# Beta in four loads spread by TensorE, L written in three operations, and conversions moved behind the rounds, in a DeltaNet and SwiGLU kernel

## The chip, the cores and the metric

The kernel runs on one core of a Trainium2 chip, as one program. The metric is the time of one execution in device microseconds (us); lower is better. The engines are named as in the profile: PE (TensorE; PEld is its loading of stationary operands), DVE (VectorE), ACT (ScalarE), POOL (GpSimd) and SP (SyncE). SP issues nearly all transfers; ACT and POOL can issue them too, each in the order of its own instructions.

## The reference, cut to what matters

The first part is a linear recurrence over 768 positions for 4 batches of 8 heads of 48 dimensions; its output, turned to 3072 tokens of 384 features, goes through a gated feed-forward block.

```python
k_n = k / (np.linalg.norm(k, axis=-1, keepdims=True) + 1e-06)
for t in range(S):
    kt, vt, bt = (k_n[:, :, t], v[:, :, t], beta[:, :, t, None])
    y[:, :, t] = np.einsum('bhd,bhde->bhe', q[:, :, t], state)
    v_old = np.einsum('bhde,bhd->bhe', state, kt)
    state = state + bt[:, :, :, None] * np.einsum('bhd,bhe->bhde', kt, vt - v_old)
...
g = x @ w_gate
silu = g * (1.0 / (1.0 + np.exp(-g)))
val = x @ w_val
return (silu * val @ w_out).astype(np.float32)
```

Everything is FP32. `beta` has one number for each batch, head and position.

## The kernel before, in words

The 768 positions are worked in 12 chunks of 64. Within a chunk the recurrence becomes a triangular system: with L the strict lower triangle of K K^T, scaled by Beta over the norms, the chunk's updates are the solution of that system. Chunks are treated in pairs, called groups. Groups 1 to 5 invert their diagonal blocks by a substitution of 31 steps on DVE (`substitute`). Group 0, chunks 0 and 1, comes first and has its own functions, which the change is about.

The order of the work is written out by hand (`tc.manual_schedule`, L1539): what stands earlier in the text is issued earlier on its engine, and each engine keeps that order. For the start it is this.

- K of chunks 0 and 1 is loaded, half by SP and half by ACT (L186, L187). `load_beta` (L383) is then called 16 times (L1549 to L1551): each loads 8 heads for one block of 32 positions of either chunk straight to the 8 lanes (partitions) that use it, with 672 numbers a lane, of which later steps read every fourth block of 32. Eight of these go out on POOL, four on ACT and four on SP.
- `first_tiles` (L553) clears L's tile and makes masks. `norms` (L359) sums squares of K.
- SP goes on with Q of chunk 0, K of 2 and 3, Q of 1, V of 0 and the first weights (L1556 to L1565).
- `unread` (L577) issues 100 products of one column, whose results nobody reads.
- `turned` (L420) makes K^T: eight transposes on PE (L444) and two copies on ACT (L446). It is called for chunk 0 and chunk 1, and then `first_gram` (L584) makes K K^T of both. For each of 32 pairs of head and batch it issues two products: the upper 32 rows against their own 32 columns (L592), and the lower 32 rows against all 64 (L593).
- `first_diag` (L596) copies diagonal blocks out, half by ACT and half by DVE; ACT copies Beta into place (L1573); DVE turns the blocks over (L1577) and `first_scale` (L612) multiplies by Beta over the norms, with POOL and DVE.
- `first_substitution` (L625) inverts diagonal blocks of 16 in 15 steps of two DVE operations (L637, L643). `first_z` (L645) and `spread_z` (L650) put the result, Z, where PE reads it.
- Meanwhile ACT runs `low_copies` (L600) for chunks 0 and 1: the part of L outside the diagonal blocks, six operations a chunk on 32 lanes each (L605, L610). PE turns Q of chunks 0 and 1 and K of 2 and 3 and makes their products (L444, L458); ACT copies results.
- `advance(0)` then runs: N = L times Z (L667), the first solution (L876), and three rounds (L896). A round multiplies by N in two halves (two parities of the heads) and adds on DVE (L1260). After that come the outputs (L932, or L896 again for chunk 0), the turning into tokens (L989, L992) and the new state (L944, L956).

The weights arrive in pieces and are rewritten before PE uses them: ACT makes two operations of each piece (`power_step`, L257) and DVE three (`convert`, L273: L282, L290, L302). The first gate products need pieces 0, 2 and 4, the first value products pieces 1, 3 and 5. Before, each of the six halves of the rounds is followed by the conversion of one of these pieces (L1615 to L1617). From L1634 on the feed-forward products of chunks 0 and 1 follow, with the rest of the conversions between them (`chain`, L1627), and from chunk 2 on a loop with fewer products a chunk (`gate_val_fast`, `output_fast`).

Of the kernel before, what the change touches and what calls it, by code (L numbers as in the profile page):

```python
# [13 lines left out]
C = 64  # L14
# [6 lines left out]
def kernel(  # L21
# [201 lines left out]
    place_of += [("z1", H_ * n) for n in (2, 3, 1, 0)]  # L223
    place_of += in_wo + in_work + (in_z1 + in_work) * 3

    beta_s = places["wo"].bitcast(FP32)[:, 6 * H_ : 6 * H_ + NG * 128]
    LATE = {"zb": 18, "p_sb": 12}
    freed_by = {}
    for n, (name, lo) in enumerate(place_of):
# [150 lines left out]
                out=beta_b[:, g], in0=beta_b[:, g], in1=r_n, op=ALU.mult  # L380
            )

    def load_beta(at, queue=nc.gpsimd):  # L383

        s_, blk, c, par = at // 8, at // 4 % 2, at // 2 % 2, at % 2
        lo, m = 64 * c + R * blk, (NG - 1) * 128 + R
        queue.dma_start(
            out=beta_s[8 * at : 8 * at + 8, 0:m],
            in_=beta.rearrange("(b bp) (j par) s -> b par bp j s", b=2, par=2)[
                s_ ^ par, par, :, :, lo : lo + m  # L390
            ],
        )

    def first_n():
        n = n_t[0].rearrange("p c h -> p (c h)")
# [157 lines left out]
    def first_tiles():  # L553
        a = work.tile([128, C * 2 * HH], FP32, name="a_sb")
        for c in range(2):
            l_sb[c] = a[:, R * R * c : R * R * (c + 1)].rearrange(
                "p (h k) -> p h k", k=C
            )
        first_of["flat"] = new_mb().rearrange("p k i -> p (k i)")
        first_of["diag"] = first_of["flat"].rearrange("p (j h) -> p h j", j=R)  # L560
        first_of["zb"] = places["z1"].bitcast(FP32)[:, 4 * H_ - 1056 : 4 * H_]
        first_of["mb"] = places["wo"].bitcast(FP32)[:, 2 * H_ : 2 * H_ + 1056]
        nc.vector.memset(first_of["zb"], 0.0)
        nc.vector.memset(a, 0.0)
        for x, rows in enumerate((slice(16, C), slice(R, C), slice(48, C), slice(0, R))):
            nc.vector.tensor_reduce(
                out=m_two[:, x],
                in_=ident.rearrange("p (b n) -> p b n", b=2)[:, :, rows],
                axis=mybir.AxisListType.X,
                op=ALU.add,  # L570
            )
        nc.vector.tensor_tensor(
            out=m_rows, in0=m_two[:, :, 0], in1=m_two[:, :, 1], op=ALU.add
        )
        nc.vector.tensor_scalar_mul(m_low, m_rows[:, 0:3], -1.0)

    def unread():  # L577

        p = ps_pair("p_t", "px")[:, 0]
        for n in range(100):  # L580
            q_ = QUADS[n % 4][0]
            nc.tensor.matmul(p[q_, 0:1], ident[q_, q_], ident[q_, 0:1])

    def first_gram(c, tag):  # L584

        p_g = ps_pair("p_g", tag)
        p_v = p_g.rearrange("p par (x h i) -> p par x h i", x=2, i=R)
        for bp, j, par, b, _ in every():
            k_v = kt[c][half_of(par), bp, j, b].rearrange("p (x i) -> p x i", x=2)
            h, s_ = NJ * bp + j, b ^ par  # L590
            hi, lo = slice(64 * s_, 64 * s_ + R), slice(64 * s_ + R, 64 * s_ + C)
            nc.tensor.matmul(p_v[hi, par, 1, h], k_v[:, 0], k_v[:, 0])  # L592
            nc.tensor.matmul(p_v[lo, par, :, h], k_v[:, 1], k_v)  # L593
        return p_v

# [3 lines left out]

    def low_copies(c, p):  # L600
        l_v = l_sb[c].rearrange("p (par h) k -> p par h k", par=2)
        for s_ in range(2):
            hi, lo = QUADS[2 * s_][0], QUADS[2 * s_ + 1][0]
            for rows, x in ((hi, 0), (lo, 2)):
                nc.scalar.mul(  # L605
                    l_v[rows, :, :, B16 * x : B16 * x + B16],
                    p[rows, :, 1, :, 0:B16],
                    m_low[rows, x : x + 1],
                )
            nc.scalar.mul(l_v[lo, :, :, 0:R], p[lo, :, 0], -1.0)  # L610

    def first_scale(r_b):  # L612
        zb, b = first_of["zb"], beta_b[:, 0]
# [925 lines left out]
    with tc.manual_schedule(  # L1539
        engines={  # L1540
            mybir.EngineType.PE,
            mybir.EngineType.Activation,
            mybir.EngineType.DVE,
            mybir.EngineType.SP,
            mybir.EngineType.Pool,
        }
    ):
        new_n(0)
        for at in range(0, 16, 2):  # L1549
            load_beta(at)  # L1550
            load_beta(at + 1, nc.sync if at % 4 else nc.scalar)  # L1551
        first_tiles()
        norms(0)

        norms(1)
        load_q(0)  # L1556
        load_k(2)
        load_k(3)
        load_q(1)
        load_v(0)  # L1560
        for n in range(12):
            stage(n)
        load_v(1)
        stage(12)
        stage(13)  # L1565
        copy_a, copy_v = nc.scalar.copy, nc.vector.tensor_copy
        unread()
        turned(0, False)
        turned(1, False, "py")
        p_g = [first_gram(0, "px"), first_gram(1, "py")]  # L1570
        first_diag(0, 0, p_g[0], copy_a)
        first_diag(0, 1, p_g[0], copy_v)
        copy_a(beta_b, beta_s.rearrange("p (g r) -> p g r", g=NG)[:, :, 0:R])  # L1573
        first_diag(1, 0, p_g[1], copy_a)
        r_b = first_n()
        first_diag(1, 1, p_g[1], copy_v)
        nc.vector.transpose(first_of["mb"][:, 0 : R * R], first_of["flat"])  # L1577
        first_scale(r_b)
        low_copies(0, p_g[0])
        turned(0, True, 0)  # L1580
        low_copies(1, p_g[1])
        turned(2, False, "px")
        first_q = [gram_steps(0, True, 2)]
        next(first_q[0])
        turned(3, False, "py")
        turned(1, True, 0)
        gram(2, False, "px", (copy_a, copy_a))
        gram(3, False, "py", (copy_a, copy_a))
        first_q.append(gram_steps(1, True, 0))
        next(first_q[1])  # L1590
        first_substitution()
        for n in range(14, 18):
            stage(n)
        first_z()
        for n in range(18, 23):
            stage(n)
        some, others = slice(0, HH // 2), slice(HH // 2, HH)
        spread_z(0, 1, nc.scalar, some)
        spread_z(0, 0, nc.vector)
        spread_z(0, 1, nc.vector, others)  # L1600
        scale_v(0)
        for steps_of in first_q:
            next(steps_of)
        new_nt(0, qpad[1].rearrange("p bp h d -> p (bp h d)"))
        zb_1 = work.tile([128, R, R], FP32, name="zb", bufs=1)
        new_nt(1, zb_1.rearrange("p k i -> p (k i)"))
        step("advance", advance, 0)
        power_step(0)
        power_step(2)
        for x in range(2):  # L1610
            spread_z(1, x, nc.scalar)
            power_step((4, 1)[x])
        power_step(3)
        power_step(5)
        for n in (0, 2, 4, 1, 3, 5):  # L1615
            step("advance", advance, 0)
            converts_first(n)  # L1617
        step("advance", advance, 0)
        p_n = banks("p_n", "px")
        n_products(1, p_n, (0,))  # L1620
        step("advance", advance, 0)
        n_products(1, p_n, (1,))
        scale_v(1)
        for par in range(2):
            n_copy(1, p_n, par)

        def chain(at):  # L1627

            step("advance", advance, 0 if steps("advance", 0) < 4 else 1)
            converts(1 + (at + 1) % 2)  # L1630

        pairs = [(c, f) for c in range(2) for f in range(0, 8, 2)]
        pairs += [(c, f) for f in range(8, FT, 2) for c in range(2)]
        for at, (c, f) in enumerate(pairs):  # L1634
            early = c == 0 and f < 4
            if c == 1 and f == 0:
                finish(1)
                second_inverse.append(invert(1))
                for _ in range(3):
                    next(second_inverse[0])  # L1640
            elif not early:
                point(2)
            need((6, 12, 18, 24, 30, 30)[f // 2])
            gate_val(c, f, fill, at, chain if early else None)
        need(len(pieces))
        for bp in range(NB):
            point(2)
            output(0, bp, fill, (4, 8))
        output(1, 0, fill, (4, 8))
        hold.clear()  # L1650
        first_blocks(True)
        first_blocks(False)
        point(2)
        output(1, 1, fill, range(2, FT, 2))
        finish(2)
        x_sums(2)
        sums_of_w(12)
        for c in range(2, NCH):
            if c > FAST:
                begin(c, 0)  # L1660
            point(c + 1)
            if c == FAST:
                begin(c, 0)
            for r in range(ROUNDS):
                gate_val_fast(c, r, fill)
            output_fast(c, fill)
            finish(c + 1)
            x_sums(c + 1)
# [30 lines left out]
```

## Time and profile before

| what | value |
|---|---|
| time, median of 4 runs | 707.93 us (706.82 to 710.69) |
| the profiled execution, its own time | 706.82 us |
| its span | 705.1 us |
| PE busy | 682.7 us, 97% of the span, 11,440 matmuls |
| DVE, ACT, POOL busy | 473.5, 261.7, 52.9 us |
| first product of the rounds (L896) begins | 37.05 us |
| first gate product (L1189) begins | 52.05 us |

The profile is one execution. Its span runs from the first instruction to the last; the time contains 1.7 us more. "Idle before" is the time an engine stood before an instruction, with what ended it behind the arrow. A matmul in FP32 shows as two pairs of LDWEIGHTS and MATMUL. In the stretch tables the columns are length, busy time of PE, PEld, DVE, ACT and POOL, each with the number of instructions in brackets, then the granted clock of PE as a share of full speed, the busy share of the DMA engines and GB/s.

### The profile page before, as it was taken

Reading aid. Unit: us, or ns where it says so; the run is one execution under the profiler, and the core shown is the slowest. Engines: PE = TensorE matmul, PEld = TensorE weight load, DVE = VectorE, ACT = ScalarE, POOL = GpSimd, SP = SyncE. Lnnn points to the kernel's source line nnn. Section 1 sums busy time; section 2 is a strip of 40 time slices with the busy share of each in tenths; the row PEclk is TensorE's granted clock in tenths of the full one; section 3 lists DMA queues with packets and bytes.
Section 4 is the critical chain, followed back from the end, with each engine's and each line's share of the span. In section 5 each row is a group of like instructions: output and inputs, shape, how many; then the busy total and the mean of one; then the engine's idle time right before and its main releaser. Section 6 shows DMA issues by size and latency. Waiting matters only on the chain.

```text
span 705.1 us, 25711 instructions
## 1 busy us (share of the span) xinstructions
PE 682.7 (97%) x11440; PEld 643.1 (91%) x11440; DVE 473.5 (67%) x1092; ACT 261.7 (37%) x548; POOL 52.9 (8%) x46
## 2 busy tenths in 40 slices
PE   6689999999999999999999999999999999999997
PEld 5688888756899999999999999999999999999997
DVE  6865689798899848987458787379855345333342
ACT  3656676203543433335223235142153132142220
POOL 7000020205000030000300000300000000000000
PEclk9889999999999999999999999999999999999999
DMA  8982716004661422365333174154141141211210
GB/s 132 249 213 70 198 48 220 1 23 84 190 128 33 99 64 70 76 113 108 67 82 82 42 131 102 26 121 85 49 106 53 30 94 61 53 63 46 68 46 23
DMA packets 144111, 62.57 MB, mean 89 GB/s; under 512 B 123136, under 2 KB 126208, under 8 KB 144000
## 3 DMA queue, kind: packets, MB, share of 16 engines
q1 hardware_dynamic: 141600, 60.27, 36.2%
q8 instruction: 90, 1.47, 0.9%
q10 hardware_dynamic: 2144, 0.48, 0.5%
q0 software_dynamic: 256, 0.17, 0.1%
q14 instruction: 21, 0.17, 0.1%
HBM read 53.82 MB, written 7.08 MB: 86 GB/s over the span
## 4 chain that ended last, share of the span: by engine, by line
PE 92%; ACT 2%; DVE 2%; issue 2%; DMA 1%; SPq 0%; DVEq 0%; ACTq 0%
PE ffn L1093 43%; PE ffn L1299 20%; PE ffn L1189 8%; PE ffn L1216 4%; PE p_g L458 3%; PE p_u L876 2%; PE p_s L944 2%; PE p_r L838 2%; PE p_y L932 1%; PE p_y L847 1%; DMA kn<-in_k_dram 1%; PE p_f L989 1%; PE ffn L896 1%; PE p_u L896 1%; PE p_j L801 1%
## 5 line engine op out<-in xcount | busy, mean ns | idle before, releaser
L1093 PE MATMUL ffn<-x_ffn,wg_sb 128*128 128x128 f32 x840 | 128.3, 275 | 0.4 <-ACT x_ffn L992 0.2
L1093 PE MATMUL ffn<-x_ffn,wv_sb 128*128 128x128 f32 x840 | 128.1, 275 | 0.0
L1093 PEld LDWEIGHTS ffn<-x_ffn,wg_sb 128*128 128x128 f32 x840 | 111.1, 192 | 0.7 <-ACT ffn L1149 0.3
L1093 PEld LDWEIGHTS ffn<-x_ffn,wv_sb 128*128 128x128 f32 x840 | 110.7, 192 | 0.0
L1123 ACT ACTIVATE sil<-ffn 128x256 f32<-128x256 f32 x120 | 46.0, 383 | 132.8 <-PE ffn L1093 128.1
L1299 PE MATMUL ffn<-wo_sb,h_f 128*128 128x192 f32 x480 | 83.4, 327 | 0.0
L1128 DVE TENSOR_TENSOR h_f<-sil,ffn 128x256 f32<-128x256 f32 x120 | 49.5, 418 | 48.6 <-ACT sil L1123 46.3
L1299 PEld LDWEIGHTS ffn<-wo_sb,h_f 128*128 128x128 f32 x480 | 78.1, 190 | 0.4
L1260 DVE TENSOR_TENSOR ffn<-ffn,p_sb 128x512 f32<-128x512 f32 x58 | 40.3, 695 | 44.3 <-ACT ffn L1149 43.2
L1093 PE MATMUL ffn<-x_t,h_f 128*128 128x128 f32 x480 | 61.1, 280 | 0.2 <-ACT ffn L1106 0.2
L1093 PEld LDWEIGHTS ffn<-x_t,h_f 128*128 128x128 f32 x480 | 56.2, 191 | 1.4 <-ACT ffn L1106 0.4
L536 DVE TENSOR_TENSOR zb<-zb,tmp 128x31 f32<-128x31 f32 (+15 forms) x155 | 53.1, 343 | 5.3
L746 POOL TENSOR_TENSOR n_b<-mb,half 128x32 f32<-128x32 f32 x5 | 30.0, 6001 | 342.8 <-DVE mb L500 342.8
L530 DVE TENSOR_TENSOR tmp<-zb,mb 128x31 f32<-128x31 f32 (+15 forms) x155 | 52.7, 340 | 4.0
L1260 DVE TENSOR_TENSOR o_sb<-o_sb,ffn 128x192 f32<-128x192 f32 x49 | 17.2, 351 | 51.2 <-PE ffn L1299 49.1
L1106 ACT COPY ffn<-ffn 128x512 f32<-128x512 f32 x30 | 17.1, 571 | 63.7 <-PE ffn L1093 57.3
L1299 PE MATMUL ffn<-last_k,h_f 128*128 128x192 f32 x200 | 35.9, 327 | 0.0
L1189 PE MATMUL ffn<-x_ffn,wg_sb 128*128 128x256 f32 x144 | 34.3, 384 | 0.0
L1189 PE MATMUL ffn<-x_ffn,wv_sb 128*128 128x256 f32 x144 | 33.8, 382 | 0.0
L1299 PEld LDWEIGHTS ffn<-last_k,h_f 128*128 128x128 f32 x200 | 32.9, 190 | 0.0
L1093 PE MATMUL ffn<-x_ffn,p_sb 128*128 128x128 f32 x216 | 30.3, 283 | 0.7 <-issue 0.7
L1189 PEld LDWEIGHTS ffn<-x_ffn,wv_sb 128*128 128x128 f32 x144 | 27.0, 190 | 3.7
(267 smaller groups left out, 1071.2 us busy)
## 6 DMA issues: line engine op xcount, KB each, us to landing
h_f<-w_s SPq DMA_DIRECT2D x60, 256.0 KB, 3.0
p_sb<-w_s SPq DMA_DIRECT2D x27, 256.0 KB, 2.7
vin<-in_v_dram SPq DMA_DIRECT2D x48, 96.0 KB, 3.2
out_dram<-o_sb SPq DMA_DIRECT2D x48, 96.0 KB, 2.3
kn<-in_k_dram SPq DMA_DIRECT2D x20, 192.0 KB, 4.6
zt<-in_moe_w_out_dram SPq DMA_DIRECT2D x6, 384.0 KB
qpad<-in_q_dram SPq DMA_DIRECT2D x36, 64.0 KB, 2.7
w_s<-h_f SPq DMA_DIRECT2D x7, 256.0 KB, 2.3
```

The source lines that it names most:

```text
L458: nc.tensor.matmul(p_v[par][half_of(b if of_q else b ^ par), bp, j], kt[c][half_of(par), bp, j, b], xt[half_of(par), bp, j, b],)
L530: nc.vector.tensor_tensor(out=t_v, in0=zb[:, 0 : j + 1, j : j + 1].to_broadcast([128, j + 1, m]), in1=mb[:, j : j + 1, j + 1 : R].to_broad ...
L536: nc.vector.tensor_tensor(out=zb[:, 0 : j + 1, j + 1 : R], in0=zb[:, 0 : j + 1, j + 1 : R], in1=t_v, op=ALU.add,)
L746: nc.gpsimd.tensor_tensor(out=n, in0=mb.rearrange("p j i -> p (j i)")[:, 0 : R * R : R + 1], in1=half, op=ALU.pow,)
L1093: nc.tensor.matmul(p[:, u], w(u), moving, start=start and u == 0, stop=True, skip_group_check=True,)
L1106: nc.scalar.copy(p_y, p_x)
L1123: nc.scalar.activation(sil[:, n].rearrange("p (i n) -> p i n", i=2), p[:, 0:2], ACTF.Silu)
L1128: nc.vector.tensor_tensor(out=h_of(c, f, j), in0=sil[:, n].rearrange("p (i n) -> p i n", i=2), in1=p[:, 2:4], op=ALU.mult,)
L1189: nc.tensor.matmul(ps[name][:, i], w_sb[:, t, (f + i) * 128 : (f + i + 1) * 128], xts[c][:, t], start=(t == 0 and i == 0), stop=(t == KT - 1),
L1216: nc.tensor.matmul(p_o, hs[c, f - f % 2][:, f % 2, bp * 128 : (bp + 1) * 128], wo_sb[:, f], start=(f == 0), stop=(f == FT - 1),)
L1260: nc.vector.tensor_tensor(out=out, in0=a, in1=b, op=ALU.add)
L1299: nc.tensor.matmul(p[x, part], a(f - f % 2)[:, f % 2], b(f), start=not begun and f == 0, stop=f == FH - 1, skip_group_check=True,)
```

## The change

- Beta is loaded by four transfers, all on POOL, each with 8 heads and all 768 positions, to 16 lanes in either half (from lanes 32 and 96 on). `spread_beta` then puts them on their lanes by eight products with pieces of the identity, each of 192 columns, and one ACT copy.
- `first_tiles` clears only columns 48 to 63 of L instead of the whole tile.
- `unread` issues 110 products instead of 100.
- `first_gram` multiplies the upper 32 rows against their own 32 columns twice over, so that both halves of the result hold something on all lanes, and `low_copies` becomes three operations a chunk on all 128 lanes.
- The order of the start: chunk 0 turned, its K K^T, Beta spread, chunk 0's diagonal copies, and only then chunk 1's turning and K K^T.
- The six halves of the rounds follow one another without conversions. Pieces 0 and 2 are converted after them, piece 4 after the output step, pieces 1, 3 and 5 after chunk 1's N products; ACT's power steps stand after `spread_z` of chunk 1.

```diff
-    beta_s = places["wo"].bitcast(FP32)[:, 6 * H_ : 6 * H_ + NG * 128]
+    beta_s = places["wo"].bitcast(FP32)[:, 6 * H_ : 6 * H_ + S]
...
-    def load_beta(at, queue=nc.gpsimd):
-
-        s_, blk, c, par = at // 8, at // 4 % 2, at // 2 % 2, at % 2
-        lo, m = 64 * c + R * blk, (NG - 1) * 128 + R
-        queue.dma_start(
-            out=beta_s[8 * at : 8 * at + 8, 0:m],
-            in_=beta.rearrange("(b bp) (j par) s -> b par bp j s", b=2, par=2)[
-                s_ ^ par, par, :, :, lo : lo + m
-            ],
-        )
+    def beta_rows(s_):
+        return slice(32 + 64 * s_, 48 + 64 * s_)
+
+    def load_beta():
+        for s_ in range(2):
+            for par in range(2):
+                at = beta_rows(s_).start + 8 * par
+                nc.gpsimd.dma_start(
+                    out=beta_s[at : at + 8],
+                    in_=beta.rearrange(
+                        "(b bp) (j par) s -> b par (bp j) s", b=2, par=2
+                    )[s_ ^ par, par],
+                )
+
+    def spread_beta(copy):
+
+        p = ps_ffn([128, NG * R], "p_b", 0)
+        x = beta_s.rearrange("p (g c blk r) -> p g c blk r", g=NG, c=2, blk=2)
+        for s_ in range(2):
+            rows = beta_rows(s_)
+            for blk in range(2):
+                for c in range(2):
+                    lanes = slice(rows.start - 16 * c, rows.start - 16 * c + R)
+                    nc.tensor.matmul(
+                        p[QUADS[2 * s_ + blk][0]],
+                        ident[rows, lanes],
+                        x[rows, :, c, blk],
+                        start=c == 0,
+                        stop=c == 1,
+                    )
+        copy(beta_b.rearrange("p g r -> p (g r)"), p)
...
-        nc.vector.memset(a, 0.0)
+        for c in range(2):
+            nc.vector.memset(l_sb[c][:, :, 48:C], 0.0)
...
-        for n in range(100):
+        for n in range(110):
...
-            nc.tensor.matmul(p_v[hi, par, 1, h], k_v[:, 0], k_v[:, 0])
+            twice = k_v[:, 0:1].to_broadcast([half_rows, 2, R])
+            nc.tensor.matmul(p_v[hi, par, :, h], k_v[:, 0], twice)
             nc.tensor.matmul(p_v[lo, par, :, h], k_v[:, 1], k_v)
...
-        for s_ in range(2):
-            hi, lo = QUADS[2 * s_][0], QUADS[2 * s_ + 1][0]
-            for rows, x in ((hi, 0), (lo, 2)):
-                nc.scalar.mul(
-                    l_v[rows, :, :, B16 * x : B16 * x + B16],
-                    p[rows, :, 1, :, 0:B16],
-                    m_low[rows, x : x + 1],
-                )
-            nc.scalar.mul(l_v[lo, :, :, 0:R], p[lo, :, 0], -1.0)
+        for x in range(3):
+            nc.scalar.mul(
+                l_v[:, :, :, B16 * x : B16 * x + B16],
+                p[:, :, x // 2, :, B16 * (x % 2) : B16 * (x % 2) + B16],
+                m_low[:, x : x + 1],
+            )
...
-        for at in range(0, 16, 2):
-            load_beta(at)
-            load_beta(at + 1, nc.sync if at % 4 else nc.scalar)
+        load_beta()
...
         turned(0, False)
-        turned(1, False, "py")
-        p_g = [first_gram(0, "px"), first_gram(1, "py")]
+        p_g = [first_gram(0, "px")]
+        spread_beta(copy_a)
         first_diag(0, 0, p_g[0], copy_a)
         first_diag(0, 1, p_g[0], copy_v)
-        copy_a(beta_b, beta_s.rearrange("p (g r) -> p g r", g=NG)[:, :, 0:R])
+        turned(1, False, "py")
+        p_g.append(first_gram(1, "py"))
...
         for x in range(2):
             spread_z(1, x, nc.scalar)
-            power_step((4, 1)[x])
-        power_step(3)
-        power_step(5)
-        for n in (0, 2, 4, 1, 3, 5):
+        for n in (4, 1, 3, 5):
+            power_step(n)
+        for _ in range(6):
             step("advance", advance, 0)
-            converts_first(n)
+        converts_first(0, 2)
         step("advance", advance, 0)
+        converts_first(4)
         p_n = banks("p_n", "px")
         n_products(1, p_n, (0,))
         step("advance", advance, 0)
         n_products(1, p_n, (1,))
+        converts_first(1, 3)
+        converts_first(5)
         scale_v(1)
```

More of the change, by code (lines that the diff above doesn't have):

```diff
@@ L587, in first_gram @@
         p_v = p_g.rearrange("p par (x h i) -> p par x h i", x=2, i=R)
+        half_rows = C
         for bp, j, par, b, _ in every():
```

## The prediction

> **What bounds it now.** Two views come first: the page's slices and queues, then the chain of waits.
>
> ```profile
> PE   6689999999999999999999999999999999999997
> ...
> PEclk9889999999999999999999999999999999999999
> ...
> q8 instruction: 90, 1.47, 0.9%
> ```
>
> From the fourth slice on, PE is busy without a break, and the granted clock is full; the diff touches nothing there. What it can win lies in the first 56 us, as an earlier arrival at that unbroken work. The last line matters too: 90 packets of 16 KB carry PE's instructions. PE executes 22,880 loads and matmuls and 149 waits, so a packet holds 256.
>
> ```profile
> 9.49 1.94 PE p_t L444 x8
> ...
> 13.31 0.72 issue
> 14.03 0.19 PE p_g L592
> ...
> 16.86 1.25 DVE wo_sb L1577
> ...
> 27.38 2.68 issue
> ...
> 33.49 2.29 issue
> ...
> 37.05 5.38 PE ffn L896 x96
> ...
> 47.22 0.56 DVE uu L1260
> 47.82 0.96 PE ffn L896 x26
> ```
>
> In this chain (start, us, what) "issue" means that PE waited for nothing the profile shows. I counted PE's instructions in the timeline at such pauses: work goes on with number 705 at 14.03, 961 at 18.15, 1473 at 30.05, 1729 at 35.78. These are 256 or 512 apart. In the DMA view the instruction packets run at 6.7, 11.5, 15.4, 20.0, 27.8 and 33.0 us, and each pause ends 1.3 to 1.6 us after such a packet has ended. So PE waits for instructions, and a new packet is asked for as the one before it is begun: 14.03 to 18.15 is 4.1 us, 30.05 to 35.78 is 5.7 (with the queues full). Number 449 was not waited for: its packet ended at 8.3, so it was there by about 9.8, and PE came at 11.4.
>
> ```profile
> 33.10:36.50 3.40, 1.07 (x54) 0.82 (x50) 0.12 (x1) 0.97 (x2) 0.00 (x0) 1.00 0.97 183
> 36.50:43.30 6.80, 6.25 (x118) 6.25 (x119) 4.58 (x12) 6.52 (x15) 0.00 (x0) 0.50 0.92 238
> 43.30:47.80 4.50, 3.62 (x112) 3.34 (x110) 4.33 (x12) 0.00 (x0) 0.00 (x0) 1.00 0.96 333
> ```
>
> These windows cover the rounds of chunk 0 (L896; columns: stretch, length, PE, PEld, DVE, ACT, POOL busy, clock, DMA). After a stretch that PE mostly idled, the clock is 0.50 for 6.8 us. There PE is the limit: the first four half rounds begin 1.7 us apart (37.05, 38.79, 40.50, 42.20). At the full clock one takes 1.0. Only then does DVE hold it up: the last three sums (L1260) begin 1.6 apart, each behind the three conversion operations of one piece.
>
> **The change, part by part.** The sum is made against the profiled execution: span 705.1, its own time 706.82, the lowest of the four; their median is 707.93, that is 1.1 more.
>
> *Beta's loads.* Sixteen become four, all on POOL. On ACT, four issues go:
>
> ```profile
> 9.43 1.07 ACT L446 COPY kt<-p_t 128x512 f32<-128x512 f32 x2 [5.66 <-DMA wo_sb<-in_beta_dram]
> ```
>
> So chunk 0's copies (L446), ready since 7.8, no longer wait till 9.43. On SP four issues go; the Q load behind them went out only at 9.37 and can now go at about 2.6, with K of chunk 2 behind it. All later SP loads move up, by up to 6 us; that gains nothing directly, since no weight is waited for before the rounds, and it fills the DMA queues during 7 to 9 us, where the packet of number 449 is in flight. POOL is free earlier, but waits for DVE until 8.62 as before. Four POOL issues end by about 5.7; with the 4.4 to 6.6 us to landing of the present ones, Beta is there by 9.6 to 11.8.
>
> *Clearing less of L* (L564, 1.76 us of DVE, becomes two small memsets): DVE then waits for K until 5.79. Nothing.
>
> *Ten more unread products and eight spreading ones.* 100 products show as 200 pairs of load and matmul, so they add 40 and 32 instructions. Number 449 now falls into chunk 0's turning (443 to 458): PE does three of its transposes and must wait until 9.8 instead of coming at 11.4. What the ACT queue gave is gone here. Number 705 is then at the end of chunk 0's K K^T, and with 4.1 us for the packet it is there at 13.9. Chunk 0's product itself fits before that: five transposes, copies of 0.6 and 128 pairs at 15 to 27 ns.
>
> *Spreading* has no row. By the nearest, 192 columns at L1299 take 174 ns a pair (83.4 us over 480). Sixteen pairs overlapping over four places as the 64x64 products do: 0.7 us. One after another at half clock: 5.6. In the order written four pairs in a row go to one place, which makes 13 steps: 2.3 at full, 4.3 at half clock. [...]
>
> *Chunk 1's turning behind it.* Before, number 705 was the first instruction of chunk 1's product, with its turning done. Now turning comes after: on ACT the copy of Beta (0.4), chunk 0's diagonal (0.6), the first copy of K^T (0.6, L446) give 18.7; then the product. Its first half multiplies 32 columns more, so 128 pairs at the 14.5 ns of L458 instead of 10.5: 1.9 us. End 20.6 against 15.58: **+5.0** on DVE's chain.
>
> *DVE's chain* (L598, L1577, L621, substitution, L647, L658) is unchanged in length, so Z is ready at 29.96 + 5.0 = 35.0. But before, Z at 29.96 was not used at once: PE stood for 1473 until 30.05 and for 1729 until 35.78. Now the last of K K^T for chunk 3 and Q's product stand there (number 1473 some 4 us after chunk 2's product begins at about 27: 31, with L458 done by 32.6), and number 1729, asked for at 31, is there by 35 to 36.5, just as N's products (L667) end. So the 2.29 us pause falls mostly into a wait that exists anyway. L667 1.5, L876 1.2, copy 0.6: rounds begin at 38.2 against 37.05: **+1.15**.
>
> *L in three operations a chunk.* ACT's 12 (8 x 0.465 and 4 x 0.57, 6.0 us) become 6 of about 0.47: 3.2 us less. It lay on the chain (L605 and L610, 20 to 22.9), but Z comes at 35 now, so it only keeps ACT out of the way. If Z came at 30, it would be worth about 2.
>
> *Rounds without conversions.* Now 37.05 to 47.82 (last output product waiting for the last sum): 10.8 us. Bare, that is seven halves: 7.2 at full clock; with the clock as now, 46.65 instead of 47.82, so 9.6. PE will still idle before Z and drop to half, but L667 and L876 (2.7 us) stand between that and the rounds and use part of the slow stretch; I leave 2.5 us of it in the rounds, 1.0 lost: 8.2. The output product starts at 38.2 + 8.2 = 46.4: **-1.4**.
>
> *Conversions after the rounds.* Pieces 0 and 2 (1.8 us for two, by 60.43 to 62.26) stand beside the output products. Piece 4 (1.15) comes behind the output copies, 2.6 us after the product starts, so at +3.8; the first gate product now comes at +4.2 (52.05). Pieces 1, 3, 5 and the V scaling end at +7.7; DVE's next work is at +8.4, behind this:
>
> ```profile
> 56.23 0.29 DVE L282 TENSOR_SCALAR h_f<-wg_sb 128x256 uint32<-128x256 uint32 x1 [4.81 <-ACT last_h L271]
> ```
>
> Those 4.81 us idle are the cover: cost 0, with 0.4 to 0.7 to spare; without the cover it is 4.1 (1.83, 1.15 and the 1.15 of piece 4). ACT's power steps keep their number and have 6 us beside the rounds.
>
> *Later stretches.* All later packet borders move by 72 instructions. Counted gaps after 88 us are 1.06 (254.8), 1.06 (352.6), 0.5 and two of 0.3: about 3 in all. Some will close and others open: 0, with 1.5 either way.
>
> Sum: 706.8 - 1.4 = 705.4; I forecast **705.2**, 2.7 under the median.
>
> [...]
>
> **Rivals.** *The early path isn't late* (0.25). If number 449 comes by 8 us, or spreading overlaps over its four places (0.7), Z comes at about 31 to 32; rounds begin near 36 and run at full clock, 7.2: 43.2, so -4.6 and 702.2. For it: fewer Beta packets, and PE asks early. Against: packets at 2.5 to 7.4 us are K's, and these stay.
>
> *PE's instructions and half clock decide: slower* (0.17). If 705 and its followers need 5.7 instead of 4.1 (+1.6), spreading runs at half clock (+1.1), L667 and L876 too (+1.1), and the rounds keep 9.6 (+1.4), the output product starts at 51.6: +3.8, 710.6. It turns slower than before once rounds begin after 39.6 at my 8.2. For it: the earlier SP loads fill the queues in which the packets stand.
>
> *The conversions were no limit* (0.13). PE at half clock is the limit for four halves of six; with rounds of 9.6 at 38.2 the product starts at 47.8, no change: 706.8 to 707.9.
>
> **How the numbers follow.** Forecast 0.45 (703 to 707.5), the others as given. About 0.5% (3.5 us) is what a measurement here tells from no change: faster means below 704.4, slower above 711.5. Faster: the first rival and 0.10 of the forecast, 0.35. Slower: 0.12, from the second (it reaches 713 with 1.5 from later stretches). Same: 0.53. The range goes from the first rival's 702.2 less 1.2 to 710.0, near the second's.
>
> **What would show it.** Right: a PE pause inside chunk 0's turning until 9 to 10 us; spreading at 14; chunk 1's product ending near 20; Z near 35 and the rounds at about 38, 8 us long, with no conversion between L1260's; no idle of DVE before its first conversion of chain 0. Wrong: chunk 1's product ending by 17, or a pause of 2 us inside the rounds, or a first gate product that waits for piece 4.

## The result and the profile after

The changed kernel takes 709.85 us (median of 51 runs, 707.26 to 712.61) against 708.63 us for the kernel before in the same comparison (79 runs): the ratio is 1.0020, with a 95% interval of 1.0012 to 1.0028. So the change makes the kernel slower by 0.2%, some 1.4 us; the forecast was 705.2. The profiled execution took 709.88 us, its span is 708.2. Lines have moved by 20 to 24 (L444 is now L465, L458 L479, L592 and L593 L616 and L617, L667 L688, L876 L897, L896 L917, L1260 L1281); spreading is L406.

From the page of the changed kernel, the slices and the queue of PE's instructions:

```profile
PE   5789999999999999999999999999999999999997
...
PEclk9979999999999999999999999999999999999999
...
q8 instruction: 90, 1.47, 0.9%
```

As before, PE's idle time lies in the first three slices. The chain of waits of the changed kernel (start, us, what):

```profile
6.57 3.29 issue
9.86 1.34 PE p_t L465 x5
11.22 1.08 ACT kt L467 x2
...
14.36 0.96 issue
15.32 0.26 PE p_g L617
15.75 1.45 PE ffn L406 x16
17.20 1.91 PE p_t L465 x8
19.13 1.08 ACT kt L467 x2
...
21.88 1.49 issue
...
25.41 1.25 DVE wo_sb L1597
...
37.49 0.78 ACT zt L677
38.32 2.22 PE p_n L688 x61
...
40.66 1.71 PE p_u L897 x61
...
42.92 7.63 PE ffn L917 x192
```

The three "issue" pauses end at PE's instructions 449, 705 and 961; in the DMA records the packets end at 8.20, 13.81 and 21.77, again 1.5 to 1.7 us before PE goes on. Chunk 1's product starts at 20.26, stops for 961, and ends at 24.1 (before: 15.6). Its diagonal is turned over (L1597) at 25.4 instead of 16.9, Z is spread by 38.5 instead of 30.0, and the rounds (L917) begin at 42.92 instead of 37.05.

The windows that answer to those of before:

```profile
36.50:43.30 6.80, 4.40 (x136) 4.25 (x137) 5.66 (x9) 2.76 (x6) 0.00 (x0) 0.51 1.05 289
43.30:47.80 4.50, 4.50 (x104) 4.50 (x102) 1.29 (x4) 4.50 (x11) 0.00 (x0) 0.60 1.03 229
47.80:51.20 3.40, 3.40 (x126) 3.40 (x124) 2.26 (x5) 1.08 (x4) 0.00 (x0) 1.00 0.07 14
```

The slow stretch (clock 0.51, then 0.60) now covers N's products and the first halves of the rounds. The last three sums show what the conversions had cost, in DVE's timeline:

```profile
48.70 0.56 DVE L1281 TENSOR_TENSOR uu<-v,ffn 128x384 f32<-128x384 f32 x1 [0.38 <-PE ffn L917]
49.64 0.55 DVE L1281 TENSOR_TENSOR uu<-v,ffn 128x384 f32<-128x384 f32 x1 [0.38 <-PE ffn L917]
50.57 0.55 DVE L1281 TENSOR_TENSOR uu<-v,ffn 128x384 f32<-128x384 f32 x1 [0.38 <-PE ffn L917]
```

They are 0.93 apart instead of 1.6, and DVE waits for PE, not PE for DVE. The first gate product comes at 55.59 (before 52.05); from there to the end it takes 652.6 us against 653.1. The moved conversions hide as forecast: DVE's idle time ahead of the next piece shrinks from 4.81 to 0.82 and does not vanish.

```profile
59.78 0.29 DVE L282 TENSOR_SCALAR h_f<-wg_sb 128x256 uint32<-128x256 uint32 x1 [0.82 <-ACT last_h L271]
```

### The profile page after: what moved, and what is told of

It is laid out like the page before. It is cut to its first block, busy times and chain, and to the rows that moved or that the text cites. A ratio compares the mean times of both kernels' runs of the same rounds, so it can differ in the third digit from the quotient of the medians.

```text
span 708.2 us, 25757 instructions
## 1 busy us (share of the span) xinstructions
PE 684.8 (97%) x11476; PEld 643.8 (91%) x11476; DVE 471.6 (67%) x1093; ACT 258.1 (36%) x542; POOL 50.8 (7%) x42
## 4 chain that ended last, share of the span: by engine, by line
PE 93%; DVE 3%; ACT 2%; issue 2%; DMA 1%; DVEq 0%; ACTq 0%
PE ffn L1114 42%; PE ffn L1320 19%; PE ffn L1210 9%; PE ffn L1237 4%; PE p_g L479 2%; PE p_u L897 2%; PE p_s L965 2%; PE p_r L859 2%; PE p_y L868 1%; PE p_y L953 1%; PE p_f L1010 1%; PE ffn L917 1%; PE p_t L465 1%; PE p_u L917 1%; PE p_j L822 1%
## 5 line engine op out<-in xcount | busy, mean ns | idle before, releaser
L1114 PEld LDWEIGHTS ffn<-x_ffn,wg_sb 128*128 128x128 f32 x840 | 111.1, 192 | 0.7 <-ACT ffn L1170 0.3
L1281 DVE TENSOR_TENSOR ffn<-ffn,p_sb 128x512 f32<-128x512 f32 x58 | 40.4, 696 | 44.6 <-ACT ffn L1170 43.5
L1281 DVE TENSOR_TENSOR o_sb<-o_sb,ffn 128x192 f32<-128x192 f32 x49 | 17.2, 351 | 51.2 <-PE ffn L1320 49.1
L1127 ACT COPY ffn<-ffn 128x512 f32<-128x512 f32 x30 | 17.1, 571 | 63.7 <-PE ffn L1114 57.3
L1320 PE MATMUL ffn<-last_k,h_f 128*128 128x192 f32 x200 | 35.9, 327 | 0.0
L1210 PEld LDWEIGHTS ffn<-x_ffn,wg_sb 128*128 128x128 f32 x144 | 26.6, 190 | 4.1 <-DVE wg_sb L302 0.4
```

What stands on the lines that cost most here:

```text
L1114: nc.tensor.matmul(p[:, u], w(u), moving, start=start and u == 0, stop=True, skip_group_check=True,)
L1127: nc.scalar.copy(p_y, p_x)
L1210: nc.tensor.matmul(ps[name][:, i], w_sb[:, t, (f + i) * 128 : (f + i + 1) * 128], xts[c][:, t], start=(t == 0 and i == 0), stop=(t == KT - 1),
L1281: nc.vector.tensor_tensor(out=out, in0=a, in1=b, op=ALU.add)
L1320: nc.tensor.matmul(p[x, part], a(f - f % 2)[:, f % 2], b(f), start=not begun and f == 0, stop=f == FH - 1, skip_group_check=True,)
```

## The experiments

Theory 1: the start loses more than the rounds win, by PE's instruction packets and by the new order. Rival A: the SP loads that moved up slow the packets. Rival B: only the order counts. Stage times below come from one profiled execution each; the changed kernel, run again, shows how far these scatter (rounds begin at 42.9 and 44.5). A verdict therefore rests on ratios to before, measured on the same chip, 0.001 being 0.7 us. "K K^T 1" is the end of chunk 1's product.

| run | order | unread | conversions | loads and L | K K^T 1 | rounds begin | ratio (95% interval) |
|---|---|---|---|---|---|---|---|
| before | old | 100 | within | old | 15.6 | 37.1 | 1 |
| changed | new | 110 | behind | new | 24.1 | 42.9 | 1.0020 (1.0012 to 1.0028) |
| changed again | new | 110 | behind | new | 25.7 | 44.5 | 1.0035 (1.0015 to 1.0055) |
| e1 | old | 100 | behind | old | 16.7 | 38.5 | 0.9978 (0.9960 to 0.9997) |
| e14 | new | 110 | within | new | 24.8 | 42.6 | 1.0060 (1.0035 to 1.0085) |
| e15 | old | 92 | within | new | 17.8 | 39.5 | 1.0020 (1.0000 to 1.0040) |
| e2 | old | 92 | behind | new | 17.0 | 37.1 | 0.9987 (0.9969 to 1.0006) |
| e13 | old | 110 | behind | new | 20.6 | 42.3 | 1.0008 (0.9989 to 1.0026) |
| e11 | spread last | 110 | behind | new | 23.2 | 42.7 | 1.0037 (1.0021 to 1.0053) |
| e7 | new, loads held | 110 | behind | new | 23.9 | 42.3 | 1.0036 (1.0023 to 1.0048) |
| e4 | new | 100 | behind | new | 22.8 | 41.5 | 1.0035 (1.0022 to 1.0048) |
| e5 | new | 50 | behind | new | 22.9 | 41.6 | 0.9988 (0.9968 to 1.0008) |
| e6 | old | 50 | behind | new | 17.0 | 35.9 | 0.9947 (0.9925 to 0.9970) |
| e12 | old | 42 | behind | new | 19.7 | 40.7 | 0.9967 (0.9946 to 0.9987) |
| e16 | old | 50, then 56 | behind | new | 19.8 | 44.2 | 1.0032 (1.0008 to 1.0057) |
| e10 | old | 50 | within | old | 17.3 | 38.2 | 0.9964 (0.9944 to 0.9984) |
| e8 | old | 50 | behind | old | 18.0 | 39.9 | 0.9947 (0.9930 to 0.9963) |
| e8 again | old | 50 | behind | old | 17.4 | 39.0 | 0.9948 (0.9929 to 0.9968) |
| e9 | old | 50, then 50 | behind | old | 18.1 | 39.9 | 0.9989 (0.9971 to 1.0007) |

**The rounds.** e1 is the kernel before with this part alone; e14 is the changed kernel with it undone (ACT's operations stay where the change puts them).

```diff
+        for _ in range(6):
+            step("advance", advance, 0)
+        converts_first(0, 2)
...
-        for n in (0, 2, 4, 1, 3, 5):
-            step("advance", advance, 0)
-            converts_first(n)
```

> The kernel before with one part of the change: six halves of the rounds without conversions, the pieces converted behind them as in the changed kernel. Theory 1 (the start lost, the rounds won): the start is untouched, so the rounds begin at 37 us as before and the last sum ends near 44.7 instead of 47.2; the gain of 2.5 us stays to the end: about 706.1, ratio 0.9965. Rival (what the rounds win is given back behind them, because the conversions and the output then stand in series): the first gate product moves by less than 1 us and the time stays at 708.0 to 708.6, ratio 0.999 to 1.

> The changed kernel with the six conversions put back between the halves of the rounds; the rest, ACT's places for its part of them too, stays. Theory 1 (the rounds' gain of about 2 us is there in the changed kernel, but smaller than the loss at the start): ratio to before 1.004 to 1.006, that is 0.002 to 0.003 above the changed kernel's 1.002. Rival (with the late start the rounds win nothing): 1.001 to 1.003.

Free rounds win in both: 0.0022 alone, 1.6 us, and 0.0025 to 0.0040 from e14 to the three measurements of the changed kernel (1.0020 and 1.0035 in the table, 1.0027 under "Loads held"), 1.8 to 2.8 us. Two more pairs of the table differ in the rounds alone: e15 to e2 gives 0.0033, e10 to e8 0.0017. So the gain is there inside the changed kernel too. In e14 the rounds take from 42.60 to the end of the last sum at 53.85, 11.3 us; in the changed kernel, with nearly the same start, from 42.92 to 51.1, 8.2. But one execution says little here, for the length of free rounds goes with the granted clock. The stretch of the rounds in e11 and in the first try of "Loads held" (e3), whose rounds have the same work:

```profile
42.68:53.83 11.15, 11.15 (x219) 10.99 (x221) 3.86 (x8) 5.93 (x14) 0.00 (x0) 0.55 0.57 152
42.59:49.59 7.00, 6.64 (x219) 6.51 (x221) 3.86 (x8) 6.03 (x14) 0.00 (x0) 1.00 0.87 228
```

At a mean clock of 0.55 free rounds take 11.2 us, as long as the 10.7 to 11.3 of the four executions with conversions (before, e10, e14, e15); at the full clock they take 7.0. In e1 the rounds begin 1.4 us later than before, behind a pause of 4.3 us at number 1473, and a packet in front of the output product (number 2241 at 46.94, PE idle for 0.9 us before it) takes back a part. The profile puts the end of that wait down to a conversion on DVE; but PE stopped at the border and went on 1.4 us after the packet had ended.

**Order, with loads and L.** e2 undoes the order and has 92 unread products, so that packet borders from Q's turning on lie where before has them; e13 undoes the order alone; e15 is e2 with the conversions put back.

```diff
-        p_g = [first_gram(0, "px")]
-        spread_beta(copy_a)
+        turned(1, False, "py")
+        p_g = [first_gram(0, "px"), first_gram(1, "py")]
...
-        turned(1, False, "py")
-        p_g.append(first_gram(1, "py"))
         first_diag(1, 0, p_g[1], copy_a)
+        spread_beta(copy_a)
```

> The changed kernel with its first products in the order of before (both chunks turned, then both K K^T), Beta spread behind them, and 92 unread products, which cancel the 32 instructions of the spreading, so that all packet borders lie where they lay before. Theory 1 (the loss is the new order together with the packet borders in it): chunk 1's product ends at 15 to 16 instead of 24.1, Z is there at 30 to 31, rounds begin at 37, and the rounds' gain shows: about 706, ratio to before 0.9965. Rival A (the SP loads moved up slow the packets): packets come 6 to 8 us after they are asked for here too, pauses before instructions 1473 and 1729 grow, rounds begin at 39 to 40, 708.5 to 709.5, ratio 1.000 to 1.001.

> The changed kernel with only the order undone: both chunks turned, both K K^T, Beta spread behind them; 110 unread products stay, so the number of instructions and all packet borders from Q's turning on are the changed kernel's. Theory 1 (order and borders in the start make the loss together): 449 still stops chunk 0's turning until 9.8, chunk 1's is done by 13.3, chunk 0's product waits for 705 until 15 and chunk 1's for 961 until 18 to 20; it ends at 18.5 to 20.5 instead of 24.1, the rounds begin at 37.5 to 40 instead of 42.9, ratio to before 0.996 to 0.999. Rival (the borders alone): chunk 1's product ends after 22 and the ratio stays at 1.001 to 1.003.

> Beta's four loads, the spreading, and L in three operations a chunk, in the order of before, with 92 unread products (all borders from Q's turning on where before has them) and the conversions back within the rounds. Theory 1 (this part is worth nothing by itself: ACT's 3.2 us are hidden): chunk 1's product ends at 15.5 to 17, rounds begin at 36 to 37.5, ratio to before 0.999 to 1.002. Rival (the shorter ACT work lets K of chunk 2 and Q be turned earlier, and Z is used earlier): 0.996 to 0.998.

Chunk 1's product answers much as Theory 1 has it, if a little late, ending at 17.0 (15 to 16 expected) and 20.6 (18.5 to 20.5). The time answers only in part. In e2 the rounds begin at 37.1 and the last sum ends at 44.4, but then the chain shows

```profile
44.67 3.08 issue
47.75 1.35 PE ffn L917 x26
```

which is the wait for number 2241, in the output product's first instructions; PE went on there 7.0 us after border 1985. In e13 number 1473 is waited for 3.6 us. ACT spreads its half of Z (L677, 36.14) only after it has copied the products that had waited, while DVE began its half at 34.13; N's products and the solution then run at half clock (0.50), so the rounds begin no earlier than 42.3, and its ratio is not told apart from the changed kernel's. Rival "borders alone" is not excluded by e13's ratio, but chunk 1's product did move by 3.5 us. e15 lies at the upper edge of what was expected: Beta's loads, spreading and L win nothing in the old order and may cost up to 0.4%; e2 against e1 and e6 against e8 put the same part at 0.0009 and 0.0000.

**Loads held.** The first try left Q's load where it was, because the cleared columns are not the loaded ones; it stands for a second look at the changed kernel (K K^T 1 at 23.9, rounds at 42.6, ratio 1.0027, 1.0012 to 1.0042). e7 holds them:

```diff
         norms(0)
+        nc.vector.memset(qpad[0][:, :, :, 0:1], 0.0)
         norms(1)
```

> The changed kernel with one thing undone: Q of chunk 0 and all SP loads behind it go out only at about 9 us, as before (a small clearing of the Q tile on POOL stands behind the first norms and holds them). Theory 1: packets still stand in the same places of PE's work, 705 is waited for until 14.5 to 15.3 and 961 until 22 to 23.4, chunk 1's product ends at 23 to 24 and the time stays within 1 us of the changed kernel's 709.85. Rival A (the early loads fill the queues in which the packets stand): 705 is there by 13.9 and 961 within 4 to 5 us of it, chunk 1's product ends at 20 to 21, the rounds begin at 39 to 40, about 706.5 to 707, ratio to before 0.997.

> The changed kernel with Q of chunk 0, and with it all later SP loads, held until DVE has done the first norms (about 8.5 us instead of 2.6; a small clearing of loaded columns of Q's tile stands there). The earlier run that was to do this did not hold them: its loads went out at 2.57 all the same, so it counts as a second look at the changed kernel. Theory 1: 449 is at 9.8 as before or a little earlier, 705 waited for until 14 to 15.3, chunk 1's product ends at 21.5 to 24, ratio to before 1.000 to 1.003. Rival A (the loads that moved up are what delays packet 961 by 8 us): 961 comes within 4 to 5 us of 705, chunk 1's product ends at 19.5 to 21, about 706.5 to 707.5, ratio 0.997 to 0.999.

SP's timeline and the chain of e7:

```profile
8.66 1.32 SPq L135 DMA_DIRECT2D qpad<-in_q_dram  x2
```

```profile
6.72 2.74 issue
...
13.96 1.77 issue
15.73 0.26 PE p_g L617
...
22.30 0.94 issue
```

Held by 6 us, the loads change nothing: 705 at 15.73, 961 at 23.2, 7.5 us apart, and no gain in time. Rival A falls: it is not the earlier start of these loads. Full DMA queues as such are not excluded, for between 705 and the packet behind it the DMA engines' share was 0.92 here and 0.95 in the changed kernel.

**Spreading.** e11 takes the spreading out from between the two products.

```diff
         p_g = [first_gram(0, "px")]
-        spread_beta(copy_a)
...
         first_diag(1, 0, p_g[1], copy_a)
+        spread_beta(copy_a)
```

> The changed kernel, 110 unread products, with Beta's spreading moved from between the two K K^T to behind both; chunk 1's turning stays behind chunk 0's product. If spreading is one part and the turning in series the other part of what the new order costs: chunk 1's product begins 1.5 us earlier than in the changed kernel, at about 18.8, and ends at 21 to 23, by when packet 961 comes: ratio to before 0.999 to 1.002. If the late packet 961 (5.3 us from border 705 to its start, 1.3 to 1.8 in the kernels with the old order) hangs on the spreading, it now starts within 3 us and chunk 1's product ends by 21; if it hangs on the turning and its wait for ACT, it starts again only as chunk 1's product begins.

Chunk 1's product starts at 19.23 (20.26) but ends at 23.2, because 961 is there at 22.69 only. The packet again began late, 4.5 us after border 705 and 1.0 us after the product began, so it doesn't hang on the spreading. The time did not fall.

**The borders moved.** e4, e5, e6, e8, e10 and e12 change the number of unread products, in the changed kernel (e4, e5), with the old order (e6, e12), and in the kernel before with (e8) and without (e10) free rounds.

```diff
-        for n in range(110):
+        for n in range(50):
```

> The changed kernel with 100 unread products instead of 110, so that every packet border comes 40 instructions later in the work: 449 in chunk 0's K K^T, 705 in the last product of the spreading, 961 at the 238th of the 256 instructions of chunk 1's K K^T. Theory 1: all eight transposes of chunk 0 run by 8, its product stops until 9.8 and ends near 11.5 instead of 14.4; 705 is still waited for until 14 to 15.3 and 961 until 20 to 23; chunk 1's product ends at 20 to 23.3: 708 to 709.5. Rival B (only the order on PE counts, not the borders): chunk 1's product moves by under 0.5 us and the time by under 0.5 from 709.85.

> The changed kernel, its order kept, with 50 unread products instead of 110: all packet borders come 240 instructions later in the work. 449 is then at the 231st of the 256 instructions of chunk 0's K K^T, 705 at the 183rd of chunk 1's, and the border that was waited for until 23.4 lies behind both. Theory 1 (the packets make the loss, the order itself only little): chunk 1's product ends at 17 to 18.5 instead of 24.1, Z is there at 31 to 32 instead of 38.5, the rounds begin at 36.5 to 38 instead of 41.5 to 43: 705 to 707.5, ratio to before 0.994 to 0.998. Rival B (spreading and chunk 1's turning standing behind chunk 0 cost it, whatever the borders): chunk 1's product ends at 21 or later and the time moves by less than 1 us from the changed kernel's.

> The changed kernel with the order of before at the start (both chunks turned, both K K^T, Beta spread behind) and 50 unread products; 449 lies in chunk 0's K K^T, 705 at the 215th instruction of chunk 1's. Theory 1: chunk 1's product ends at 13.5 to 15.5 (17.0 with 92 unread products), Z at 28 to 30, rounds begin at 34 to 36, and 704 to 706.5 if no packet takes it back behind the rounds: ratio to before 0.992 to 0.997. Rival B gives the gain of the order alone, that of the run with 92: 0.9987. If a packet in front of the output product takes 3 us, as in the run with 92, 708.

> The kernel before with the rounds free of conversions and 50 unread products instead of 100; nothing else of the change. All packet borders come 200 instructions later in the work: 449 in chunk 0's K K^T, 705 at the 175th instruction of chunk 1's. Theory 1: chunk 1's product ends at 13.5 to 15.5 (16.7 with 100), rounds begin at 33.5 to 36 (37.05 with 100): 704.5 to 707 on a chip where before has 708.6, ratio 0.994 to 0.997. Rival (the borders matter only by chance of the later ones): no better than the same with 100, ratio 0.998 or above.

> The kernel before with 50 unread products instead of 100 and nothing of the change. Theory 1 (packet borders and the rounds add up): the late stops go from about 1.9 to 0.8 us, the start loses about as much as the run with 50 and free rounds showed (chunk 1's product ends at 17 to 18 instead of 15.6), ratio 0.996 to 0.999. Rival (the gain needs the free rounds): 1.000 or above.

> The changed kernel with the order of before at the start and 42 unread products, 8 fewer than in the run with 50 (ratio 0.9947): with the 32 instructions of the spreading all later packet borders then lie where they lie in the kernel before with 50 unread products, whose late stops add up to 0.8 us, against 2.8 in that run. Theory 1a (late borders count): the late stops fall by 2 us, ratio 0.991 to 0.994, 703 to 704.5 where before has 708.6. Theory 1b (only the first 20 us count): 0.994 to 0.996, no difference to 50.

The stage times miss nearly everywhere. In e5 chunk 1's product ends at 22.9, not 18: the first packet (for 449) now began at 10.8 instead of 6.7 us, perhaps because the instructions just behind border 193 wait for K (not tested), and PE stopped 2.6 us in chunk 0's product and 2.1 in chunk 1's. e6 and e8 end it at 17.0 and 18.0, not at 15. With 42, border 193 itself comes at 8.7 and chunk 1's product ends 2.7 us later than with 50. e4 gains nothing. Of the ratios, those of e6, e8 and e10 are as Theory 1 has it, those of e4, e5 and e12 lie above what was expected. Rival B has e5's product right (21 or later), but not its time (0.9988 against 1.0020). Yet with 50 the times fall: 50 instead of 92 to 110 is worth 0.0031 to 0.0040 in four pairs (e8 against e1, e5 against the changed kernel, e10 against before, e6 against e2), 2.2 to 2.8 us, by one number and with no work saved on the path at the start. So the gain is not where I looked for it.

**Behind the rounds?** e9 and e16 leave 50 at the start and issue more after Q's first turning (in e8 the chain that ends last has no work of PE from 18.1 to 25.4 us there), which moves only the later borders.

```diff
-        unread()
+        unread(50, ps_pair("p_t", "px")[:, 0])
...
         turned(0, True, 0)
+        unread(50, ps_ffn([128, 512], "p_t", 2))
```

> The kernel before with rounds free of conversions and 50 unread products at the start, as in the earlier run, but with the other 50 issued a little later, between the turning of Q of chunk 0 and of K of chunk 2, where PE stands idle. From there on all packet borders lie where they lie with 100 at the start. Theory 1a (what 50 unread products win comes from the packet borders after the rounds, where PE is without a break: short stops at 170 to 355 us add up to 2.3 us with 100 and to 0.8 with 50): the stops come back and the time is that of 100, ratio to before 0.997 to 0.999. Theory 1b (it comes from the borders in the first 20 us): the time stays at that of 50, ratio 0.994 to 0.996.

> The changed kernel with the old order and 50 unread products at the start (ratio 0.9947 in the earlier run), and 56 more behind Q's first turning, where PE stands idle: they move only the later borders, to where the kernel before has them with 50, whose late stops add up to 0.8 us instead of 2.8. Theory 1a (late borders count): the start as in the earlier run, first gate product at 50.5 to 52.5, late stops below 1.2 us, ratio 0.991 to 0.994. Theory 1b (they don't): 0.994 to 0.996; if the added products themselves come onto the path, 0.996 to 0.998.

In e9 the start is e8's (first gate product at 53.5 and 53.6) and the gain goes: 0.9989 against 0.9947. PE's timeline of e9 has stops that e8's lacks, such as

```profile
256.98 0.27 PE L814 MATMUL p_j<-t,z 32*32 32x32 f32 x9 [0.80 <-issue]
...
354.74 0.49 PE L1092 MATMUL ffn<-x_ffn,p_sb 128*128 128x128 f32 x2 [0.60 <-issue]
```

This speaks for the later borders. e16 speaks against a simple rule: its ratio is 1.0032, its first packet came at 11.0 us (8.5 in e6, same instructions up to there), and PE's pauses of 1.7, 3.7, 2.4, 1.2 and 2.7 us delay the rounds to 44.2.

**Again.** The best kernel (e8) and the changed one, unchanged.

> The kernel before with free rounds and 50 unread products once more, unchanged (ratio 0.9947, 0.993 to 0.9963, in the earlier run). If the ratio is the kernel's own: 0.993 to 0.997, late stops again 0.8 us within 0.4, chunk 1's product ending at 17 to 19. If it was a lucky stretch of runs: 0.997 to 0.999, the sum of the rounds' gain alone.

> The changed kernel once more, unchanged (ratio 1.002 in the earlier runs). Theory 1: packet 961 again starts 4.5 to 5.5 us behind border 705, chunk 1's product ends at 23 to 25, the rounds begin at 41 to 43.5; ratio 1.001 to 1.004. If the late packet was a chance of the one execution: chunk 1's product ends at 20 to 22.

Both ratios come back. The stops do not: e8's late stops (PE's "issue" stops of 0.2 us or more behind the first gate product) add up to 0.8 us in one execution and 2.2 in the other, at the same ratio, with the first gate product at 53.6 and 52.0. In all twenty executions the time from the first gate product to the end, less these stops (0.8 to 3.8 us), is 650.7 to 651.9 us. So what one execution takes is settled by when that product comes and by these stops, and both change from one execution of a kernel to the next. So the late stops of one execution do not explain the gain of 50 unread products; what does stays open. In the changed kernel packet 961 came late again (PE 9.1 us behind 705), so that is no chance of one execution.

## Why the prediction was wrong, step by step

- **"there at 13.9 (4.1 per packet)"**: 705 came at 15.32, 5.5 us after 449. The pause until 9.8 inside chunk 0's turning was right (9.86).
- **Spreading**: the sum has it done at 17.1 (18.7 less ACT's copies of 1.6), which leaves it 3.2 us from 13.9 on. No run shows this 3.2; spreading took 1.5 us here (15.75 to 17.20), at a granted clock of 1.00. Too dear, so that it was done at 17.2, as forecast, is luck. (13 steps at half clock make 4.5 us by the row used, not 4.3.)
- **"the first copy of K^T ... give 18.7; then the product"**: 20.26. The sum has ACT's copies of 1.6 us behind the spreading, but not the eight transposes (1.9) and both copies (1.1) that stand in series there. This is the step that failed by working: the transposes were listed as moved and not priced.
- **"End 20.6 ... +5.0"**: 24.1, +8.5. 1.6 from the step before; the rest is the product, 3.8 us instead of 1.9, of which 1.49 is the wait for 961. That border was not looked at: 4.1 a packet would have brought it at 19.4, in time; it took 8.0.
- **"rounds begin at 38.2 ... +1.15"**: 42.9, +5.9, and 42.3 to 44.5 in the other executions with this start. (The terms add up to 38.3.) Pauses of before did absorb some of the delay, 2.6 us instead of the 3.85 reckoned with; N's products and the solution took 2.2 and 1.7 at a clock of 0.50 instead of 1.5 and 1.2.
- **Rounds 8.2, -1.4 at the output product**: 8.2 in the profiled execution, as forecast, 2.6 shorter than before; but they end 3.3 us later than before, at 51.1. The 8.2 is in part luck: the clock was half until 46.9, for 4.0 us of the rounds and not 2.5, and the same kernel took 7.0 us in e3 and 11.0 when run again, where the clock was half at 40.3 to 43.7 and 47.1 to 53.9 and a packet was waited for 1.7 us. What free rounds are worth was measured alone (1.6 us) and within the changed kernel (1.8 to 2.8).
- **L in three operations, hidden**: right that it wins nothing; loads, spreading and L together cost 0 to 0.4% (e15).
- **Conversions hidden; later stretches 0 ± 1.5**: right for the profiled execution (0.82 us of idle time left; 0.5 us less from the gate product on). The 3 us of gaps counted in the prediction are 1.9 by the profile's idle times.

The second rival's course, "PE's instructions and half clock decide", is what happened in the main: packets above 5 us, L688 and L897 slow (clock 0.50), rounds beginning after 39.6. It was given 0.17 and priced at 710.6; the profiled execution took 709.88. That its price is so near is in part luck: its spreading at half clock (1.5 measured) and its rounds of 9.6 us (8.2) did not come, and the transposes in series and the wait for 961, which did, are not in it. Its reason, the SP loads moved up, is refuted by e7. In the first 50 us PE pauses for 0.96 to 3.29 us at three borders in a row here, and for 4.31 at one in e1. Behind 50 us, at some 80 borders, it stops for 0.2 us or more only twice here (0.65 and 0.54) and three times before (0.87, 0.69 and 0.30). The profile's difference (3.1 us) is larger than that of the medians (1.2), since the profiled execution of before was the fastest of its four.

What is shown: free rounds win; the rest of the change loses more (e14, 1.0060); when SP's loads go out plays no part; turning and copies in series and packets 705 and 961 are where chunk 1's product loses. With 50 unread products the order alone is worth 0.0041 (e6 against e5, on the same chip: medians of 706.1 and 708.7 us). With 110, the changed kernel's number, how the loss splits between order and borders is only argued, for e13, which undoes the order alone, is not told apart from the changed kernel in time.

## What to carry to other kernels

Before reordering or adding even a few dozen small PE instructions in a stretch that waits on latencies, count the instructions to the next packet borders (one every 256 here, as at 449, 705 and 961) and ask which product each border falls into; price a packet by the slowest seen (here 9.1 us from border to border, where 4.1 had been taken). An operation that moves behind another one brings its whole chain with it (transposes, copies), and each link has to be priced. A number that takes no work off the path, like the 50 unread products here (0.9947 and 0.9948 with the free rounds and nothing else of the change, faster than both kernels), is worth a try by itself, by ratios over several runs, even where what it wins by stays open, as here.

## What the runs showed of the hardware that was not expected

- The time from PE's going on at border 705 (449 in e5) to the DMA of the next packet falls into two kinds. It is 1.3 to 2.9 us in ten executions, all of the old order, and 4.5 to 6.8 us in the eight of the new order (e11 included) and in e12 and e16; in the eight the DMA began 0.1 to 1.9 us after chunk 1's product did. What PE goes on with does not settle it: e6 and e16 have the same PE instructions there, and 2.9 and 5.0 us. The DMA engines' share was 0.69 to 1.16 in the first kind and 0.85 to 1.04 in the second. The cause stays open.
- Products that nobody reads count too: 50 one-column products fewer, 200 instructions, moved the time by 0.36% (e10, interval 0.9944 to 0.9984). By what way stays open.
- Two executions of the changed kernel differ by 5 us (709.9 and 715.1) and by 1.5 us at the begin of the rounds; the packet for 961 ended at 21.8 and 23.6.
